# Wider filler matmuls, two feed-forward passes moved earlier in the second chunk, and three passes of a second product moved ahead of a between-product

## The chip, the cores and the metric

The kernel runs on one core of a Trainium2 chip. The metric is the device time of one execution in microseconds (us). The engines are PE (TensorE, with its weight loads shown apart as PEld), DVE (VectorE), ACT (ScalarE), POOL (GpSimd) and SP (SyncE, which here only issues DMAs).

## The reference, cut to what matters

There are 4 batches, 8 heads, 768 tokens and 48 dimensions a head. A delta-rule attention runs over the tokens; its outputs, 384 wide, go through a feed-forward layer with 2048 hidden columns, two slopes instead of a plain ReLU, and 384 output columns. Everything is float32.

```python
k_n = k / (norm(k) + 1e-06)
for t in range(S):
    kt, vt, bt = k_n[:, :, t], v[:, :, t], beta[:, :, t, None]
    y[:, :, t] = einsum('bhd,bhde->bhe', q[:, :, t], state)
    v_old = einsum('bhde,bhd->bhe', state, kt)
    state = state + bt[..., None] * einsum('bhd,bhe->bhde', kt, vt - v_old)
h = x @ w_in                                  # x: y as (3072, 384)
g = maximum(h, 0) + alpha * minimum(h, 0)
out = g @ w_out
```

## The kernel before, in words

**Tiling.** The tokens are cut into 12 chunks of 64. One *step* handles one chunk of one pair of batches, so there are N = 24 steps, numbered from 0: steps 0 and 1 are the first chunk, 2 and 3 the second, 4 and 5 the third. Inside a chunk the recurrence is solved as a triangular system. Its 64 x 64 inverse is built of 32 x 32 blocks: DVE inverts the diagonal blocks of four steps (NJ = 4) at once by elimination (`eliminate`, lines 516 and 522, with transposes by `turns`, line 489), ACT places them (`placing`, lines 642, 648 and 659) into the tiles `diag` and `inv`, and PE multiplies them together in two *between-products*: `between_1`, whose result ACT copies into `mid`, and `between_2`, which completes `inv` (lines 709 and 722 for the second chunk, where a DVE add, line 729, reads the second product out of PSUM; line 674 from step 4 on, where ACT copies, line 686).

**A step's other work.** `flips` transposes keys and queries on PE (line 377; ACT copies them out, line 398). `grams` multiplies keys with keys (line 424; DVE scales them, line 430). `through_state` (763), `query` (748), `solve` (788), `outputs` (801), `next_state` (817) and `to_ffn` (840) follow, with DVE reading most results. These products use a ring of three double PSUM banks, `p_pair`, in turn (`ps_big`): a product that comes to a bank waits until the last reader of what was there is done.

**Feed-forward.** Once a chunk's two steps are done, `ffn_in(c)` makes the hidden tiles (line 931): 48 matmuls a chunk, three to a hidden tile of 128 columns, two hidden tiles to one of two PSUM banks `p_ffn`. After every sixth matmul ACT (line 941) and DVE (two instructions, line 943) apply the slopes. `ffn_out(c)` is the second product for chunks 0 and 1 (line 973): two halves u of 128 tokens, each the sum of 16 matmuls f of 384 columns in one `p_ffn` bank, copied out by ACT (line 979) and stored. These are generators: each `next` issues one matmul, here called a *pass*. In the trace a float32 matmul leaves two records.

**Order.** All engines' order is the order in which the program writes the work (`manual_schedule`); `weave` interleaves generators by shares, and each engine takes its instructions in that order. Places that matter here:

- `busy` (line 1391) issues filler matmuls into an unused PSUM bank: the operands are the identity and a transposed-key tile `k_t[3]`, 112 rows of each. Their results are read by nothing. They stand where PE would wait: `busy(8)` ahead of the first chunk's elimination result, shorter ones within `first_chunk`.
- `second_pair` does steps 2 and 3, with `alongside(p, ...)` issuing p passes of `ffn_in(0)` and some weight conversions between its products. Weights come in by DMA as 32-bit words and are rebuilt by ACT (225, 226) and DVE (235, 240).
- After `second_pair`: `ffn_in(1)` beside `eliminate(1)`; then `ffn_out(0, True)`, whose two halves take turns; then a `weave` of `prelude(4)` (both between-products of step 4), `catch_up` (grams and flips of steps 10 and 11) and the first 8 passes of `ffn_out(1)`; then two rounds of `attention(n)`, n = 4 and 5, each with 12 more passes.
- From step 6 (`JOINED`) on, the rest of the feed-forward (`tail`) fills PE between the attention products up to the end.

Of the kernel before, what the change touches and what calls it, by code (L numbers as in the profile page):

```python
# [36 lines left out]
EARLY = 8  # L37
FIRST = 6
# [5 lines left out]
def kernel(  # L44
# [18 lines left out]
    FT = DFF // 128  # L63
# [17 lines left out]
    def ps_one():  # L81
        return ps_big()[:, 0]
# [17 lines left out]
    def ps_ffn():  # L100
        turn[0] ^= 1
        return ffn_banks[turn[0]]

    def half(i):
        return slice(64 * i, 64 * i + 64)
# [5 lines left out]
    ROWS = C + D  # L111
# [4 lines left out]
    def padded(name, n):  # L116

        ts = [const.tile([128, H, C], FP32, name=f"{name}{i}") for i in range(n)]
        for t in ts:
            nc.gpsimd.memset(t[:, :, D:C], 0.0)  # L120
        return ts

    NKE, NKL, NQ = 3, 2, 2
    ident = const.tile([128, 128], FP32, name="ident")
    make_identity(nc, ident)
    k_early, k_late, q_pad = padded("ke", NKE), padded("kl", NKL), padded("qp", NQ)
# [12 lines left out]
    def load_early(n, *queues):  # L139
        if n < N:  # L140
            fetch(k, n, early(n)[:, :, 0:D], *queues)
# [189 lines left out]
    stats, k_t, q_t, a_t = {}, {}, {}, {}  # L331
# [76 lines left out]
    def now(pieces):  # L408
        for x in pieces:
            x()  # L410
# [40 lines left out]
    NJ = 4  # L451
# [174 lines left out]
    def placing(n, parts, by_vector=False):  # L626


        if n >= N:
            return  # L630
        m, j = n // NJ, n % NJ
        first, second = slice(0, HB), slice(HB, C)
        own = slice(j * H, j * H + H)

        def put(dst, cols, src, i):
            out, x = dst[n % NE][:, :, cols], src[m][:, own]
            if by_vector:
                nc.vector.tensor_scalar(
                    out=out, in0=x, scalar1=which[:, i : i + 1], scalar2=None, op0=ALU.mult
                )  # L640
            else:
                nc.scalar.mul(out, x, which[:, i : i + 1])  # L642

        if 0 in parts:
            if n < NJ:
                put(diag, first, turned, 0)
            else:
                nc.scalar.copy(diag[n % NE][:, :, first], turned[m][:, own])
            yield
        if 1 in parts:  # L650
            put(inv if n >= NJ else diag, second, inverse, 1)
            yield
        if 2 in parts:
            put(inv, first, inverse, 0)
            yield
        if 3 in parts:
            w = stats[n][1]
            for t in range(2):
                nc.scalar.copy(w[half(1 - t), 2], w[half(t), 1])
            yield  # L660
# [300 lines left out]
    def ffn_out(c, together=False):  # L961

        gs = gss.pop(c)
        p_o = {}
        if together:
            order = [(u, f) for f in range(FT) for u in range(2)]
        else:
            order = [(u, f) for u in range(2) for f in range(FT)]
        for u, f in order:
            assert len(out_done) > f  # L970
            if f == 0:
                p_o[u] = ps_ffn()[:, 0:DM]
            nc.tensor.matmul(
                p_o[u], gs[f // 2][:, f % 2, u * 128 : (u + 1) * 128], w_out[:, f],
                start=(f == 0), stop=(f == FT - 1),
            )
            if f == FT - 1:
                o_sb = work.tile([128, DM], FP32, name="o_sb")
                nc.scalar.copy(o_sb, p_o[u])
                store(c, u, o_sb)  # L980
            yield
# [299 lines left out]
    IN_PARTS, OUT_PARTS, FAST_PARTS = FT * KT, NB * FT, 7 * FP // 2  # L1281


    def part(gen, n):
        for _ in range(n):
            next(gen, None)
            yield

    def weave(*gens):

        live = []
        for i, (g, n, *at) in enumerate(gens):
            at = at[0] if at else 0.0
            live.append([at, i, (1.0 - at) / n, g])
        while live:
            live.sort(key=lambda x: (x[0], x[1]))
            at = live[0]
            at[0] += at[2]
            try:
                next(at[3])  # L1300
            except StopIteration:
                live.pop(0)
# [83 lines left out]
    def busy(n, p=None):  # L1386

        p = ps_one() if p is None else p
        while n > 0:
            x = p[:, 0 : int(512 * min(n, 1))]  # L1390
            nc.tensor.matmul(  # L1391
                x, ident[0:ROWS],
                k_t[NJ - 1].rearrange("p g i -> p (g i)")[0:ROWS, 0 : x.shape[-1]],
            )
            n -= 1

# [103 lines left out]
    fetch_out, _, conv_out = weights(pieces, stages, ids, out_done)  # L1500
    PARTS_OUT = 2 * len(pieces)

    def chain(*gens):
        for g in gens:
            yield from g
# [46 lines left out]
    def alongside(products, pieces, *gens):  # L1552
        weave((part(first_in, products), products), (part(convert_on, pieces), pieces), *gens)

    def second_pair():

        n = 2
        both, x = (n, n + 1), NJ
        halves = [cross(0, slice(i * H, i * H + H), edge, half_way) for i in both]
        squares(x)  # L1560
        alongside(4, 2)
        for h in halves:
            next(h)
        flips(x, n)
        load_early(x + NKE)
        load_q(n + 2)
        squares(x + 1)
        alongside(5, 2)
        next(halves[0])
        flips(x + 1, n + 1)  # L1570
        load_early(x + 1 + NKE)
        load_q(n + 3)
        now(weigh(x))
        place(n, (0,))
        alongside(4, 2)
        next(halves[1])
        now(weigh(x + 1))
        place(n + 1, (0,))
        alongside(4, 2)
        for i in both:  # L1580
            now(between_1(i))
        now(grams(x))
        squares(x + 2)
        alongside(5, 3, (chain(*(placing(i, (1, 2, 3)) for i in both)), 6))
        for i in both:
            now(between_2(i))
        now(grams(x + 1))
        for i in both:
            scale_v(i)
        flips(x + 2, N)  # L1590
        load_early(x + 2 + NKE)
        now(weigh(x + 2))
        alongside(5, 3)
        y = ps_big()
        pieces = []
        for i in range(2):
            pieces += through_state(n + i, None, y[:, :, i * G * D : (i + 1) * G * D])
        now(pieces)
        squares(x + 3)
        alongside(5, 3)  # L1600
        y = ps_big()
        pieces = []
        for i in range(2):
            pieces += solve(n + i, y[:, :, i * G * D : (i + 1) * G * D])
        now(pieces)
        now(grams(x + 2))
        flips(x + 3, N)
        load_early(x + 3 + NKE)
        now(weigh(x + 3))
        alongside(5, 2)  # L1610
        pieces = []
        for i in both:
            y = ps_big()
            pieces += outputs(i, y[:, :, 0 : G * D]) + next_state(i, y[:, :, G * D : 2 * G * D])
        now(pieces)
        for i in both:
            load_late(i + 2)
            load_v(i + 3)
        alongside(5, 2)
        for i in both:  # L1620
            to_ffn(i)
        now(grams(x + 3))
        alongside(IN_PARTS - 42, 1)

    second_pair()
    fetch_out(len(stages))
# [15 lines left out]
    def prelude(n):  # L1642
        place(n, (0,))
        now(between_1(n))
        yield
        place(n, (1, 2))
        yield
        now(between_2(n))
        yield
        place(n, (3,))  # L1650
        scale_v(n)
        place(n + 1, (0,))
        yield

    def catch_up():
        for n in range(FIRST + NJ, EARLY + NJ):
            now(grams(n))
            flips(n + 1, N)
            squares(n + 1)
            yield  # L1660
            now(weigh(n + 1))
            load_early(n + 1 + NKE)
            yield

    late = ffn_out(1)
    few = OUT_PARTS // 4
    weave((prelude(NJ), 4), (catch_up(), 2 * (EARLY - FIRST), 0.1), (part(late, few), few))

    def feed_forward():
        for c in range(2, FAST_IN):  # L1670
# [26 lines left out]
    for n in range(NJ, JOINED):  # L1697
        extra = [] if n == NJ else [(weight_sums(0, 0, 3), 3)]
        weave(
            (attention(n), SHARES), (placing(n + 1, (1, 2, 3)), SHARES * PLACING),  # L1700
            (part(late, (OUT_PARTS - few) // 2), (OUT_PARTS - few) // 2),
            (part(blocks, share), share), *extra,
        )

    PIECES_OF = {JOINED: (2, 3, 2 * PIECES), JOINED + 1: (4, 4, 7)}
    TURNS = [(3, 3, 4), (3, 3, 4), (4, 4, 4), (0, 5, 6)]
    FILL = {JOINED: (8, 12, 12), JOINED + 1: (10, 12, 10), JOINED + 2: (8, 10, 12)}
# [2 lines left out]
    for n in range(JOINED, N):  # L1710
        if n == LATE:
            banks(2, 2)
        fill, share = FILL.get(n, FILLS[n % 2]), PIECES_OF.get(n, TURNS[n % NJ])
        extra = [[], [], []]
# [72 lines left out]
```

## Time and profile before

| what | us |
|---|---|
| runs | 666.2, 670.96, 676.8; median 670.96 |
| profiled execution, whole | 664.06 |
| profiled execution, span | 662.3 |
| PE busy in the span | 641.2 |
| mean granted TensorE clock over the span | 0.994 |
| DVE busy / ACT busy | 492.2 / 264.8 |

Times within the trace count from the start of the span. A profile line of the timeline has start, length, engine, source line, operation, output and inputs, and how many instructions were merged; in square brackets is the idle time of the engine before it and what ended that. The windows view gives for each stretch the busy time of each engine, the granted clock and the DMA share.

### The profile page before, as it was taken

What the parts mean: (1) busy time and instruction counts of PE and PEld (TensorE: products, weight loads), DVE (VectorE), ACT (ScalarE), POOL (GpSimd) and SP (SyncE); (2) the same over time, 40 slices, a digit from 0 to 9 for tenths busy, and PEclk for the clock granted to TensorE, in tenths of its full rate; (3) what the DMA queues carried; (4) which work ended last, traced back from release to release, by engine and by line L of the source; (5) the groups of instructions that cost most, each with busy time, mean ns of one, the idle gap of its engine ahead of it and who ended that gap; (6) DMA issues with size and microseconds to landing.
All of it is one profiled execution on the core that took longest, in us unless ns stands there. A gap on an engine that the chain in (4) does not pass through costs nothing.

```text
span 662.3 us, 22128 instructions
## 1 busy us (share of the span) xinstructions
PE 641.2 (97%) x9551; PEld 567.0 (86%) x9551; DVE 492.2 (74%) x1180; ACT 264.8 (40%) x621; POOL 93.7 (14%) x201
## 2 busy tenths in 40 slices
PE   4999999989999999999999999999999999999997
PEld 3578888557688998998998998988999999999997
DVE  5955889868999859748859758858968658567383
ACT  5937765245454343243343233232245245042140
POOL 6000122001000000001000000000035044062260
PEclk9799999999999999999999999999999999999999
DMA  8848845211422122122111111112111210100000
GB/s 121 245 126 218 199 87 144 49 37 38 78 58 50 21 55 50 26 50 51 26 38 37 27 38 37 26 38 38 26 42 34 44 32 2 31 9 2 24 1 25
DMA packets 110962, 37.72 MB, mean 57 GB/s; under 512 B 104160, under 2 KB 107248, under 8 KB 110864
## 3 DMA queue, kind: packets, MB, share of 16 engines
q1 hardware_dynamic: 109088, 35.81, 24.8%
q8 instruction: 75, 1.23, 0.8%
q10 hardware_dynamic: 1776, 0.49, 0.4%
q14 instruction: 23, 0.19, 0.1%
HBM read 31.56 MB, written 4.72 MB: 55 GB/s over the span
## 4 chain that ended last, share of the span: by engine, by line
PE 83%; DVE 10%; ACT 3%; SPq 2%; issue 1%; DMA 0%; DVEq 0%; ACTq 0%
PE p_ffn L931 22%; PE p_ffn L995 17%; PE p_more L1247 8%; PE p_more L1163 4%; PE p_ffn L1153 3%; PE p_ffn L1247 3%; PE p_pair L377 2%; PE p_ffn L1158 2%; PE p_pair L763 2%; PE p_pair L788 2%; PE p_pair L674 2%; PE p_pair L801 2%; DVE prod L516 2%; DVE block L522 2%; PE p_pair L1391 2%; PE p_pair L424 1%
## 5 line engine op out<-in xcount | busy, mean ns | idle before, releaser
L931 PE MATMUL p_ffn<-xt,w_in 128*128 128x256 f32 x768 | 175.1, 382 | 2.3 <-DVE act L943 1.2
L931 PEld LDWEIGHTS p_ffn<-xt,w_in 128*128 128x128 f32 x768 | 142.7, 190 | 22.7 <-issue 1.9
L943 DVE SCALAR_TENSOR_TENSOR act<-act,al_t,p_ffn 128x256 f32<-128x256 f32 x112 | 48.6, 476 | 29.3 <-ACT act L941 29.2
L941 ACT ACTIVATE act<-p_ffn 128x512 f32<-128x512 f32 x56 | 33.3, 594 | 81.3 <-PE p_ffn L931 81.2
L522 DVE TENSOR_TENSOR block<-block,prod 128x30 f32<-128x30 f32 (+9 forms) x150 | 49.9, 333 | 5.2
L1187 POOL TENSOR_TENSOR k_t<-k_t 128x128 f32<-128x128 f32 (+1 forms) x48 | 29.5, 615 | 166.6 <-ACT k_t L1182 164.1
L516 DVE TENSOR_TENSOR prod<-block 128x30 f32<-128x30 f32 (+9 forms) x150 | 49.0, 326 | 1.8
L995 PE MATMUL p_ffn<-w_out,act 128*128 128x192 f32 x288 | 49.6, 328 | 0.1
L995 PEld LDWEIGHTS p_ffn<-w_out,act 128*128 128x128 f32 x288 | 46.5, 190 | 0.8 <-issue 0.5
L842 ACT COPY xt<-p_pair 128x384 f32<-128x384 f32 x22 | 10.4, 478 | 91.2 <-PE p_pair L840 77.5
L366 POOL TENSOR_TENSOR beta_t<-beta_t,rec 128x8 f32<-128x8 f32 x24 | 6.3, 261 | 284.6 <-DVE rec L364 264.7
L1187 POOL TENSOR_TENSOR block<-block 128x128 f32<-128x128 f32 (+1 forms) x48 | 27.9, 582 | 16.7 <-ACT block L1182 14.2
L1153 PE MATMUL p_ffn<-xt,w_in 128*128 128x256 f32 x96 | 28.7, 380 | 0.0
L773 DVE TENSOR_TENSOR r<-v_raw,p_pair 64x192 f32<-64x192 f32 (+1 forms) x66 | 23.2, 352 | 1.1
L686 ACT COPY inv<-p_pair 32x256 f32<-32x256 f32 x40 | 14.5, 362 | 23.9 <-DVE u L792 23.6
L792 DVE TENSOR_TENSOR u<-p_pair,wgt 128x384 f32<-128x384 f32 x24 | 13.3, 557 | 14.3 <-PE p_pair L674 14.0
L1201 DVE SCALAR_TENSOR_TENSOR act<-block,al_t,act 128x256 f32<-128x256 f32 x32 | 19.1, 637 | 5.2 <-ACT block L1197 5.1
L1015 DVE TENSOR_TENSOR o_sb<-u,p_ffn 128x192 f32<-128x192 f32 x24 | 7.9, 351 | 20.2 <-PE p_ffn L995 19.7
L1247 PE MATMUL p_more<-w_out,act 128*128 128x192 f32 x128 | 21.9, 329 | 0.0
L642 ACT ACTIVATE inv<-inverse,which 128x256 f32<-128x256 f32 x44 | 21.6, 503 | 0.3
L1182 ACT COPY k_t<-p_more 128x512 f32<-128x512 f32 x16 | 9.4, 586 | 30.6 <-PE p_more L1163 25.9
L752 ACT COPY y<-p_pair 128x384 f32<-128x384 f32 x22 | 10.4, 478 | 27.5 <-PE p_pair L748 25.5
(224 smaller groups left out, 1415.5 us busy)
## 6 DMA issues: line engine op xcount, KB each, us to landing
w_out<-in_moe_w_in_dram SPq DMA_DIRECT2D x12, 512.0 KB, 5.2
qp<-in_q_dram SPq DMA_DIRECT2D x48, 96.0 KB, 3.0
v_raw<-in_v_dram SPq DMA_DIRECT2D x48, 96.0 KB, 2.9
kl<-in_k_dram SPq DMA_DIRECT2D x96, 48.0 KB, 2.8
out_dram<-o_sb SPq DMA_DIRECT2D x92, 48.0 KB, 1.6
space_out<-in_moe_w_out_dram SPq DMA_DIRECT2D x11, 384.0 KB, 5.2
ke<-in_k_dram SPq DMA_DIRECT2D x43, 96.0 KB, 3.3
w_out<-in_moe_w_out_dram SPq DMA_DIRECT2D x5, 384.0 KB, 4.0
```

The lines of the kernel that those rows point to most:

```text
L516: nc.vector.tensor_tensor(out=prod, in0=r[:, 0:j, j : j + 1].to_broadcast([128, j, n]), in1=r[:, j : j + 1, j + 1 : HB].to_broadcast([128, ...
L522: nc.vector.tensor_tensor(out=r[:, 0:j, j + 1 : HB], in0=r[:, 0:j, j + 1 : HB], in1=prod, op=ALU.add)
L642: nc.scalar.mul(out, x, which[:, i : i + 1])
L773: nc.vector.tensor_tensor(out=r[to, a], in0=v_in[to, a], in1=p[own, a, :, 0:D], op=ALU.subtract)
L931: nc.tensor.matmul(p_h[:, i], w_in[:, t, (f + i) * 128 : (f + i + 1) * 128], xt[:, t], start=(t == 0), stop=(t == KT - 1),)
L941: nc.scalar.activation(g, p_h, ACT.Relu, scale=-1.0)
L943: nc.vector.scalar_tensor_tensor(out=g[:, i], in0=g[:, i], scalar=al_t[:, f + i : f + i + 1], in1=p_h[:, i], op0=ALU.mult, op1=ALU.add,)
L995: nc.tensor.matmul(p, x(i), w(i), start=(i == 0), stop=(i == FP - 1))
L1153: nc.tensor.matmul(p[:, f * 256 : f * 256 + 256], w(2, f), xt[:, 2], start=True, stop=False)
L1163: nc.tensor.matmul(q[:, j], a, b, start=True, stop=True)
L1187: nc.gpsimd.tensor_tensor(out=dst, in0=a, in1=b, op=ALU.add)
L1247: nc.tensor.matmul(p, x(i), w(i), start=(i == 0), stop=(i == FP - 1))
```

## The change

Four edits. The fillers read all 128 rows of the identity and of `k_late[0]`, the tile that holds the keys of step 0 (and later of the even steps) for `next_state`. In `second_pair` seven passes instead of five stand between `between_1` and `between_2` of steps 2 and 3, and two fewer at its end. `ffn_out(0, True)` takes its last four matmuls in the order (half 0, f 14), (half 0, f 15), (half 1, f 14), (half 1, f 15). Three passes of `ffn_out(1)` are issued ahead of `prelude`, `prelude` gives way one time fewer (the placing of `inv` now follows `between_1` at once), and the two rounds of attention get 11 passes each instead of 12; the last of all 33 calls only ends the generator.

```diff
@@ ffn_out
         if together:
-            order = [(u, f) for f in range(FT) for u in range(2)]
+            order = [(u, f) for f in range(FT - 2) for u in range(2)]
+            order += [(u, f) for u in range(2) for f in range(FT - 2, FT)]
@@ busy
             nc.tensor.matmul(
-                x, ident[0:ROWS],
-                k_t[NJ - 1].rearrange("p g i -> p (g i)")[0:ROWS, 0 : x.shape[-1]],
+                x, ident, k_late[0].rearrange("p h d -> p (h d)")[:, 0 : x.shape[-1]]
             )
@@ second_pair
-        alongside(5, 3, (chain(*(placing(i, (1, 2, 3)) for i in both)), 6))
+        alongside(7, 3, (chain(*(placing(i, (1, 2, 3)) for i in both)), 6))
...
-        alongside(IN_PARTS - 42, 1)
+        alongside(IN_PARTS - 44, 1)
@@ prelude
         now(between_1(n))
-        yield
         place(n, (1, 2))
@@
-    few = OUT_PARTS // 4
-    weave((prelude(NJ), 4), (catch_up(), 2 * (EARLY - FIRST), 0.1), (part(late, few), few))
+    few, rest = OUT_PARTS // 4, 11
+    for _ in part(late, OUT_PARTS - few - 2 * rest + 1):
+        pass
+    weave((prelude(NJ), 3), (catch_up(), 2 * (EARLY - FIRST), 0.1), (part(late, few), few))
@@ attention rounds
-            (part(late, (OUT_PARTS - few) // 2), (OUT_PARTS - few) // 2),
+            (part(late, rest), rest),
...
+    assert next(late, None) is None
```

## The prediction

> **What bounds the kernel now.** I read the page's busy times first, then PE's waits, then the windows, then the timeline around the edited places.
>
> ```profile
> PE 641.2 (97%) x9551; PEld 567.0 (86%) x9551; DVE 492.2 (74%) x1180; ACT 264.8 (40%) x621; POOL 93.7 (14%) x201
> ```
>
> PE has 21.1 us of idle time in 662.3, of which 8.8 lie in the first 16 us (the windows view: 7.19 busy). The waits from there on that matter are in PE's list (total us, times, longest):
>
> ```profile
> PE p_pair L674 <- ACT diag L648: 1.4, 1, 1.4
> PE p_ffn L931 <- DVE act L943: 1.2, 1, 1.2
> PE p_pair L840 <- DVE y L807: 1.1, 1, 1.1
> PE p_pair L674 <- ACT inv L642: 0.9, 1, 0.9
> PE p_pair L722 <- ACT diag L642: 0.9, 2, 0.7
> ```
>
> The change aims at the first (step 4's first between-product), the fourth (its second) and the fifth (steps 2 and 3): 1.36, 0.89 and 0.65 + 0.22 us. That is 3.1 us, the most that the moved passes can fill. The windows (length, busy us of PE, PEld, DVE, ACT, POOL, clock, DMA) say who sets the pace behind them:
>
> ```profile
> 20.00:22.00 2.00, 2.00 (x3) 0.90 (x4) 1.74 (x7) 2.00 (x5) 0.00 (x0) 0.50 1.03 420
> 24.00:26.00 2.00, 2.00 (x6) 0.81 (x6) 1.72 (x8) 1.93 (x5) 0.00 (x0) 1.00 1.27 234
> ...
> 75.00:97.00 22.00, 22.00 (x413) 18.99 (x404) 18.67 (x46) 14.10 (x32) 3.29 (x8) 1.00 0.64 174
> ...
> 165.00:190.00 25.00, 23.45 (x392) 17.42 (x391) 23.12 (x58) 12.48 (x33) 0.56 (x2) 1.00 0.44 84
> 190.00:215.00 25.00, 23.65 (x350) 20.55 (x350) 24.62 (x56) 11.29 (x29) 2.55 (x4) 1.00 0.24 43
> 215.00:240.00 25.00, 25.00 (x435) 23.77 (x436) 18.86 (x55) 7.65 (x20) 1.41 (x4) 1.00 0.21 41
> ```
>
> PE alone sets 75 to 97. From 165 to 215 it is **DVE**, busy 47.7 of 50 us, and PE's two waits there (1.1 and 1.2) are for DVE. From 215 on it is PE. The timeline of steps 2 and 3:
>
> ```profile
> 65.04 2.42 PE L931 MATMUL p_ffn<-xt,w_in 128*128 128x256 f32 x10
> ...
> 68.11 1.12 PE L722 MATMUL p_pair<-diag,mid 64*64 64x32 f32 x32 [0.65 <-ACT diag L642]
> ...
> 69.35 0.42 DVE L729 TENSOR_TENSOR inv<-diag,p_pair 128x256 f32<-128x256 f32 x1 [0.67 <-PE p_pair L722]
> ...
> 69.81 0.40 ACT L659 COPY wgt<-wgt 64x4 f32<-64x4 f32 x2
> ...
> 71.00 0.65 PE L377 MATMUL p_pair<-ident,ke 128*112 128x128 f32 x4
> ...
> 72.65 0.58 ACT L941 ACTIVATE act<-p_ffn 128x512 f32<-128x512 f32 x1
> ...
> 73.83 0.86 DVE L943 SCALAR_TENSOR_TENSOR act<-act,al_t,p_ffn 128x256 f32<-128x256 f32 x2
> ```
>
> To be seen: L377 follows L729 in the PSUM bank, and L941 with its two L943 now comes after both.
>
> [...] with 256 columns the fillers of 112 rows have a median of 431 ns, the hidden matmuls of 128 rows a mean of 382. [...] PE idles 3.43 us up to 16.06 (for `al_sb`), the clock is 0.50 from 17.5 to 22, then 1.00 from 24 on. [...]
>
> **Part A, fillers of 128 rows: 0.** Same number, same columns. The first filler now waits for the four loads of `k_late[0]`: issued from 10.69 to 14.15, landing at most 4.0 us after issue, so by 18.2; it starts at 19.73. The last filler (to 46.8) now holds back the reload of that tile, where L817 (to 44.4) did; but SP is issuing weights until 49.43 and comes to that load at 49.52. Both covers hold. Unknown is the clock in executions that were not profiled; see the rivals.
>
> **Part B, seven passes: +0.3.** A pass of L931 takes 0.43 us (14 records in 3.29 against 10 in 2.42). Two fill the idle 0.65 before L722 and push it to about 68.3. The second L722 is released by ACT at 69.4 as before, so its 0.22 goes too. At the end of the following grams, 71.0, PE has done two passes more: −0.87. But 4 + 5 + 4 + 4 + 7 = 24 passes end the fourth bank, so L941 and two L943 are now issued here, ahead of both L729. ACT reaches L941 when the last L659 ends, 69.81 + 0.40 = 70.21, to 70.8; L943 takes 0.87, to 71.7; the first L729 ends at 72.1 instead of 69.77. L377 waits for it: 72.15 instead of 71.00, +1.15. Sum +0.28. Who is behind the waiting L729: the grams' L430, L737 and `through_state`'s L773, about 0.8 late; `solve` (L788, 78.70) moves to 79.9 and finds them done near 79.2. PE is full up to 97, so +0.3 is carried; `flips` at 115.05, and through ACT and DVE the elimination from 119.55, move with it. Bounds: −0.87 (no new wait) to +1.2 (nothing filled).
>
> **Part C, three passes ahead of step 4: −0.3.** A pass of L973 takes 0.65 (64 records, 32 passes, in 20.93). Three take 1.95 where 1.36 is idle, so the first L674 starts 0.6 late. They need the bank of half 0: with the new order its last matmul ends two passes (1.3) before the end, and the 0.48 copy is done in time; by the old order the copy ended at 137.16, about when PE came free, so the reordering is worth 0 to 0.1. The removed yield puts the placing of `inv` (2 x 0.45) right behind the `mid` copies (0.74) on ACT instead of behind L477, L398 and L347: done at about 141.6, while PE comes near 143.3, so the 0.89 goes. Net −0.3 at the second grams (145.68). From there L430, ACT L477 and the L489 transposes of the next elimination move by −0.3, and DVE's dense queue carries just that to 209. Whatever PE gains beyond it in 150 to 209, it waits out: three passes fewer in the two rounds leave up to 1.95 of holes at L788, L801 and the step-6 products. On SP the four stores of half 0 go ahead of the `kl` load for step 6 (158.96): some 1.5 us late, needed at 200.10. Bounds: −2.25 (both waits gained, nothing given back) to +0.6.
>
> **Sum.** 0 + 0.3 − 0.3 = 0 against the profiled execution: span 662.3, whole 664.1. That execution lies 6.9 below the median of 670.96 and below all three runs; the mean of the four is 669.5. No view shows what the others lose. I predict **670 us**, between mean and median.
>
> **Rivals.**
> - *A warmer clock.* The cold stretch costs: L593 starts at 28.62, behind slow fillers, though its transposes ended at 26.48, so 2.1 us. If the other executions have more such stretches and 128 rows prevent them, up to the 6.9 go: 664 to 668. For: the spread of 10.6 us. Against: from 24 on the clock was 1.00 with 112 rows[...]. 0.12.
> - *All idle gained.* B gives −0.87, C −2.25: 670 − 3.1 = 667. For: the waits are real. Against: DVE at 95% behind them. 0.13.
> - *Slower: the slopes jam DVE.* L943 ahead of L729 is one mechanism: every 0.1 that ACT is later at L941 than 70.2 is 0.1 on L377. It decides from 69.9 on, where B turns from gain to loss. If ACT's weight rebuilding pushes L941 to 71.5, B is +1.6, and the late L773 takes L788 with it, another 1: 670 + 2.6 = 672.6, and with C's holes not absorbed (+0.6) 673. 0.17.
> - *Cold fillers.* [...] the 20.4 us of PE work between 28 and 50 run at half clock, +13 or more: 683. 0.03.
>
> **Numbers.** Forecast 0.55, the rivals as given. The forecast's own range is the spread of the runs, about 666 to 676, with ±1 for the bounds: 665 to 677. To hold eight in ten over all cases I take 663 to 678. A measurement of this kernel tells about 2%, 13.4 us, from no change; only the cold rival reaches that: faster 0.03, same 0.92, slower 0.05.
>
> **What would show it.** B: L943 before L729, L377 idle about 1.2 for L729, no wait at the first L722. C: no wait at either L674 near 139 to 143, a longer wait at L788 or L801 between 163 and 180, the wait at 208 still there. A: clock 1.00 from 24 on. The prediction is wrong if PE's idle sum falls by over 2 us, or if the clock row differs.

## The result and the profile after

| | before | after |
|---|---|---|
| median of 20 runs each, us | 670.22 (664.22 to 676.89) | 666.76 (663.75 to 670.88) |
| ratio, 95% interval | | 0.9977 [0.9958, 0.9996] |
| profiled execution, whole / span | 664.06 / 662.3 | 665.83 / 664.1 |
| from the start to the first L931 | 48.09 | 49.67 |
| from the L931 ahead of L722 (steps 2 and 3) to the L377 of the third chunk near 92 | 26.73 | 26.87 |
| from the first L973 to the first L995 (974 and 996 after) | 96.13 | 95.64 |
| from there to the end | 449.81 | 449.86 |

No difference of 2%; the forecast of 670 (663 to 678) holds. The interval of the ratio, 0.04 to 0.42%, is 0.3 to 2.8 us. Ratios leave out runs over 1.5% longer than the fastest of their kernel (4 of E8's 22, 2 of E3's 14), while medians hold all runs.

The last four rows are read from the timeline as differences between the first instructions of a line. The edits of parts B and C show in the rows of 26.73 and of 96.13 us. The stretch from the L377 near 92 us to the first L973 and the one from the first L995 to the end repeat to 0.1 us in all the traces taken here. The row of 26.73 is less steady, since stretches at half the clock (in E3 the clock is 0.82 from 64 to 68 us and 0.75 from 68 to 72) and stalls (idle time of PE for which the profile names no cause, 1.15 us in E3) can fall into it; its pieces, in the section on E6, are steady. The span of the changed kernel is longer only because it was 2.1 us late at 67 us, ahead of parts B and C (1.6 of it at the first L931).

PE's list of waits, after (total us, times, longest):

```profile
PE p_ffn L931 <- ACT beside L400: 1.5, 1, 1.5
...
PE p_ffn L931 <- DVE act L943: 1.2, 1, 1.2
PE p_pair L788 <- DVE a_t L444: 1.1, 2, 0.8
PE p_pair L377 <- DVE inv L729: 0.9, 1, 0.9
...
PE p_pair L801 <- DVE u L792: 0.7, 1, 0.7
...
PE p_pair L840 <- DVE y L807: 0.5, 1, 0.5
```

The two waits of L674 and that of L722 are gone. In their place stand L377 for L729, L788 and L801 for DVE, and the first line, L931 for the copy L400 of ACT, at 190.65 us: it was 0.25 before and is 1.54 now. L931 for L943 and L840 for L807 are old ones. The timeline of steps 2 and 3, after (L722 has no bracket left):

```profile
67.16 3.29 PE L931 MATMUL p_ffn<-xt,w_in 128*128 128x256 f32 x14
...
70.38 2.26 PE L722 MATMUL p_pair<-diag,mid 64*64 64x32 f32 x61
...
72.24 0.59 ACT L941 ACTIVATE act<-p_ffn 128x512 f32<-128x512 f32 x1
...
72.86 0.87 DVE L943 SCALAR_TENSOR_TENSOR act<-act,al_t,p_ffn 128x256 f32<-128x256 f32 x2 [2.06 <-ACT act L941]
73.64 0.75 DVE L729 TENSOR_TENSOR inv<-diag,p_pair 128x256 f32<-128x256 f32 x2
74.12 0.65 PE L377 MATMUL p_pair<-ident,ke 128*112 128x128 f32 x4 [0.92 <-DVE inv L729]
```

DVE sat idle for 2.06 us. The first L722 had ended at about 71.5, but L729, which reads its result, stood in DVE's queue behind L943, and L943 waited for L941. Both L729 come after it, and L377 after them. Step 4, after:

```profile
139.24 2.10 PE L974 MATMUL p_ffn<-w_out,sums 128*128 128x384 f32 x6
...
141.27 0.69 PE L674 MATMUL p_pair<-diag,right 32*32 32x32 f32 x32
...
142.78 0.91 ACT L642 ACTIVATE inv<-inverse,which 128x256 f32<-128x256 f32 x2
...
145.24 0.69 PE L674 MATMUL p_pair<-inv,mid 32*32 32x32 f32 x32
```

Three passes stand ahead of the first L674, and ACT has placed `inv` 1.5 us before the second one comes. What follows, in windows with the columns as before:

```profile
165.00:190.00 25.00, 22.17 (x443) 16.69 (x435) 22.80 (x58) 10.85 (x29) 1.12 (x4) 1.00 0.40 75
190.00:215.00 25.00, 23.02 (x344) 19.84 (x345) 24.62 (x55) 13.02 (x34) 2.55 (x4) 1.00 0.26 49
```

From 165 to 215 DVE is as busy as it was (47.42 of 50 us). PE's idle time there is 2.83 + 1.98 = 4.81 us, and was 1.55 + 1.35 = 2.90: 1.91 more, nearly the 1.95 of the three passes that were taken from there. The largest piece of it is the wait of L931 for ACT. ACT stands behind DVE there: its copy L477 waits for DVE's L430, and L400 follows in ACT's order.

```profile
187.61 0.82 ACT L477 COPY same<-right 32x256 f32<-32x256 f32 x2 [3.45 <-DVE right L430]
...
189.96 0.60 ACT L400 COPY beside<-p_pair 112x512 f32<-112x512 f32 x1
...
190.65 3.69 PE L931 MATMUL p_ffn<-xt,w_in 128*128 128x256 f32 x16 [1.54 <-ACT beside L400]
```

L430 comes 1.77 us later than before (186.83 against 185.06), and L931 1.77 later (190.65 against 188.88): PE has less to do ahead of it, but comes no sooner than DVE lets it.

### The profile page after: what moved, and what is told of

Read it like the earlier page. It is cut to its first block, busy times and chain, and to the rows that moved or that the text cites. A ratio compares the mean times of both kernels' runs of the same rounds, so it can differ in the third digit from the quotient of the medians.

```text
span 664.1 us, 22126 instructions
## 1 busy us (share of the span) xinstructions
PE 643.9 (97%) x9551; PEld 568.9 (86%) x9551; DVE 493.3 (74%) x1180; ACT 264.0 (40%) x621; POOL 93.2 (14%) x201
## 4 chain that ended last, share of the span: by engine, by line
PE 86%; DVE 7%; ACT 4%; issue 1%; DMA 1%; ACTq 0%; SPq 0%; DVEq 0%
PE p_ffn L931 22%; PE p_ffn L996 17%; PE p_more L1248 8%; PE p_more L1164 4%; PE p_ffn L974 4%; PE p_ffn L1154 3%; PE p_ffn L1248 3%; PE p_pair L377 3%; PE p_ffn L1159 2%; PE p_pair L763 2%; PE p_pair L788 2%; PE p_pair L801 2%; PE p_pair L424 2%; PE p_pair L674 2%; PE p_pair L1392 2%; PE p_pair L748 1%
## 5 line engine op out<-in xcount | busy, mean ns | idle before, releaser
L931 PE MATMUL p_ffn<-xt,w_in 128*128 128x256 f32 x768 | 175.1, 382 | 3.6 <-ACT beside L400 1.5
L931 PEld LDWEIGHTS p_ffn<-xt,w_in 128*128 128x128 f32 x768 | 142.7, 190 | 24.0 <-ACT beside L400 1.9
L943 DVE SCALAR_TENSOR_TENSOR act<-act,al_t,p_ffn 128x256 f32<-128x256 f32 x112 | 48.6, 476 | 30.4 <-ACT act L941 30.3
L941 ACT ACTIVATE act<-p_ffn 128x512 f32<-128x512 f32 x56 | 33.3, 595 | 81.0 <-PE p_ffn L931 80.8
L1016 DVE TENSOR_TENSOR o_sb<-u,p_ffn 128x192 f32<-128x192 f32 x24 | 7.9, 352 | 20.2 <-PE p_ffn L996 19.8
L349 DVE TENSOR_REDUCE norm<-ksq 128x8 f32<-128x384 f32 x24 | 13.0, 547 | 12.5 <-ACT ksq L347 12.4
L1202 DVE SCALAR_TENSOR_TENSOR act<-k_t,al_t,act 128x256 f32<-128x256 f32 x32 | 21.7, 718 | 0.1
```

What stands on the lines that cost most here:

```text
L931: nc.tensor.matmul(p_h[:, i], w_in[:, t, (f + i) * 128 : (f + i + 1) * 128], xt[:, t], start=(t == 0), stop=(t == KT - 1),)
L941: nc.scalar.activation(g, p_h, ACT.Relu, scale=-1.0)
L943: nc.vector.scalar_tensor_tensor(out=g[:, i], in0=g[:, i], scalar=al_t[:, f + i : f + i + 1], in1=p_h[:, i], op0=ALU.mult, op1=ALU.add,)
L1202: nc.vector.scalar_tensor_tensor(out=g[:, f], in0=r[:, f], scalar=al_t[:, 2 * i + f : 2 * i + f + 1], in1=g[:, f], op0=ALU.mult, op1=ALU.add,)
```

## The experiments

Twelve kernels. E1 to E4 take the parts one by one, E6, E7, E8, E11 and E12 alter the changed kernel, E5, E9 and E10 turn to what the fillers' rows do. The kernel before was run beside them in three sets: medians 667.77 (59 runs), 667.17 (43) and 667.23 (57). None of them shows the 670.22 of the first set again, and the 666.76 of the changed kernel lies 0.4 to 1.0 us below them where the first set had 3.5; but it was not run again beside them.

### E1 to E4: the parts alone

**E1**, part A: only the operands of `busy` changed.

> The kernel before with the 128-row fillers alone. Theory of the record [...]: ratio to before 1.000, within 0.002, and the same spread of times and granted clocks as before. Rival (wider fillers wake the clock sooner, which is where the 0.23% of the whole change came from): ratio near 0.998, the mean granted clock of the runs higher than that of before, no run above 672 us.

**E2**, parts B and C: everything but the operands of `busy`.

> The whole change but the fillers, which keep 112 rows. Theory of the record, with the sizes of the two traces: seven passes +0.1 to +0.3 us, passes ahead of step 4 -0.3 to -0.5 us, together -0.4 to 0: ratio 0.9994 to 1.000. Rival (all of the gain is in the moves): ratio near 0.9977, -1.5 us.

**E3**, part B: only the two counts of `alongside`.

```diff
-        alongside(5, 3, (chain(*(placing(i, (1, 2, 3)) for i in both)), 6))
+        alongside(7, 3, (chain(*(placing(i, (1, 2, 3)) for i in both)), 6))
...
-        alongside(IN_PARTS - 42, 1)
+        alongside(IN_PARTS - 44, 1)
```

> Only the seven passes between the between-products of steps 2 and 3. Theory: the new wait of L377 for L729 (about 0.9 to 1.2 us) takes back the filled idle time (0.87): +0.1 to +0.3 us, ratio 1.000 to 1.0005. Rival (the fill pays and the wait is hidden): -0.9 us, ratio 0.9987, and no wait of L377 for L729 in the profile.

**E4**, part C: `ffn_out`'s order, `prelude` without its first yield, three passes ahead, 11 in each round.

> Only the passes ahead of step 4, with the reordered end of the product before and the shorter prelude; fillers of 112 rows, five passes in step 2 and 3. Theory: both waits of L674 (1.4 and 0.9 us) are gone from the profile, new waits of L788 and L801 for DVE of 1 to 2 us stand between 163 and 180, net -0.3 to -0.5 us, ratio 0.9993 to 0.9996. Rival (both waits are gained and nothing is given back): -2.25 us, ratio 0.9966.

| | ratio, 95% interval | median | L931 to L377 | L973 to L995 |
|---|---|---|---|---|
| E1: A | 0.9995 [0.9965, 1.0024] | 668.29 | 27.30* | 96.73* |
| E2: B and C | 0.9985 [0.9961, 1.0009] | 667.08 | 27.54* | 95.71 |
| E3: B | 0.9963 [0.9931, 0.9995] | 666.93 | 27.36* | 96.10 |
| E4: C | 0.9988 [0.9961, 1.0016] | 666.87 | 26.74 | 95.65 |

\* a stretch at half the clock lies in this segment.

The ratios can't tell the parts apart. E3's lies further below 1 than that of the whole change, and its interval leaves 1 out, though none of its segments holds a gain. So one interval without 1 among twelve is no proof of a gain here. The segments can: C alone is worth 95.65 − 96.13 = −0.48, and in E2 it is −0.42. B can't be read from this segment in E2 or E3, where half-clock stretches fall into it. For A the profile of E1 says more than its ratio:

```profile
19.64 7.13 PE L1391 MATMUL p_pair<-kl,ident 128*128 128x512 f32 x16
27.93 1.57 PE L593 MATMUL p_pair<-turned,sums 32*32 32x16 f32 x128 [1.15 <-DVE turned L489]
29.42 1.97 PE L1391 MATMUL p_pair<-kl,ident 128*128 128x512 f32 x2
```

Sixteen records took 7.13 us, 0.45 each, at the full clock; the next two took 1.97. The window of 28 to 32 us has a clock of 0.70, that of 32 to 36 one of 0.50: it fell at about 29.6, when PE had waited 1.15 us for L489 and run the 128 small products of L593 (1.57 us). Fillers of 128 rows did not prevent that.

### E6: six passes instead of seven

```diff
-        alongside(7, 3, (chain(*(placing(i, (1, 2, 3)) for i in both)), 6))
+        alongside(6, 3, (chain(*(placing(i, (1, 2, 3)) for i in both)), 6))
...
-        alongside(IN_PARTS - 44, 1)
+        alongside(IN_PARTS - 43, 1)
```

> The whole change with six passes between the second chunk's between-products instead of seven, the seventh given back to the stretch after the grams. 4 + 5 + 4 + 4 + 6 = 23 passes do not end the fourth bank, so L941 and L943 stay behind the L729. Theory (the two ends of step B cancel: 0.87 idle filled, about the same lost to the wait of L377 for L729): no wait of L377 for L729, 0.2 to 0.3 us left at the L722, and the stretch from the L931 ahead of that L722 to the second chunk's L377 near 92 us takes 26.2 to 26.4 us, against 26.73 before and 26.87 with seven. Rival (PE loses the 0.4 elsewhere, by ACT or DVE): 26.7 or more. The ratio of the whole changes by less than 0.1%.

Ratio 0.9987 [0.9960, 1.0014], median 667.37. Its timeline:

```profile
65.96 2.86 PE L931 MATMUL p_ffn<-xt,w_in 128*128 128x256 f32 x12
...
69.04 1.12 PE L722 MATMUL p_pair<-diag,mid 64*64 64x32 f32 x32 [0.22 <-ACT diag L642]
...
71.93 0.65 PE L377 MATMUL p_pair<-ident,ke 128*112 128x128 f32 x4
```

L377 has no wait left, and each of the two groups of L722 waits 0.22. From the L931 to L377 it takes 5.97 us, as before, with one pass more in it. The segment took 26.62, above the expected 26.2 to 26.4. The ten records of L931 ahead of L840 put 0.3 into it (2.73 us, 2.43 before), with such a stall of 0.43 in their weight loads; E8 and E12 with the same six passes took 26.31 and 26.29.

Stalls and half-clock stretches come and go in this segment (seven passes took 26.87 in the change, but 27.30 in E7 and 29.07 in E11). Two pieces of it hold what the passes change, and they repeat wherever no half-clock stretch falls into them:

| passes | traces | L931 to L377 | L840 to the next L377 |
|---|---|---|---|
| 5 | before, E4, E5, E9, E10 | 5.93 to 5.97 | 4.50 |
| 6 | E6, E8, E12 | 5.94 to 5.97 | 4.07 |
| 7 | change, E7, E11 | 6.94 to 6.96 | 3.63 to 3.64 |

So six passes gain 0.4 where seven lose 0.1: the seventh, which closes the bank and calls L941 and L943, costs 0.55 net.

### E7 and E11: what carries part C

**E7** is the changed kernel with the yield of `prelude` put back:

```diff
         now(between_1(n))
+        yield
         place(n, (1, 2))
...
-    weave((prelude(NJ), 3), (catch_up(), 2 * (EARLY - FIRST), 0.1), (part(late, few), few))
+    weave((prelude(NJ), 4), (catch_up(), 2 * (EARLY - FIRST), 0.1), (part(late, few), few))
```

> The whole change with the yield of the prelude put back (and its weight of 4), so that ACT places the inverse behind the others' work again. Theory (of step C's 0.48 us the second L674's wait is the larger part): the second L674 waits 0.3 to 0.9 us for ACT's L642, and the stretch from the first L973 to the first L995 takes 95.9 to 96.1 us, against 95.64 with the change and 96.13 before. Rival (the passes ahead of step 4 alone bring it, or DVE's dense queue behind takes back whatever is gained here): 95.6 to 95.7.

Ratio 1.0011 [0.9985, 1.0038], median 667.65. The timeline of ACT and of the second L674 in E7:

```profile
147.93 0.82 ACT L477 COPY same<-right 32x256 f32<-32x256 f32 x2 [1.66 <-DVE right L430]
148.77 0.58 ACT L398 COPY k_t<-p_pair 112x512 f32<-112x512 f32 x1
149.38 0.52 ACT L347 ACTIVATE ksq<-ke 128x384 f32<-128x384 f32 x1
149.81 0.89 ACT L642 ACTIVATE inv<-inverse,which 128x256 f32<-128x256 f32 x2
150.35 0.69 PE L674 MATMUL p_pair<-inv,mid 32*32 32x32 f32 x32 [0.89 <-ACT inv L642]
```

The wait is back at 0.89, and the segment takes 96.52: 0.88 more than with the change, and 0.39 more than before. That is beyond both expectations. The moved passes without the yield's removal lose, and removing the yield gains 0.88 on top of them, as the pieces show:

| from, to | before | E7 | change |
|---|---|---|---|
| L973, first L674 | 22.29 | 22.68 | 22.67 |
| first L674, L763 of step 4 | 10.17 | 10.17 | 9.22 |
| L763, L377 near 160 | 11.45 | 11.46 | 11.55 |
| L377, first L995 | 52.22 | 52.21 | 52.20 |

The removal without the moved passes was not run; by these pieces it would be worth about 0.9, an estimate.

**E11** is the changed kernel with `ffn_out`'s old order.

```diff
-            order = [(u, f) for f in range(FT - 2) for u in range(2)]
-            order += [(u, f) for u in range(2) for f in range(FT - 2, FT)]
+            order = [(u, f) for f in range(FT) for u in range(2)]
```

> The whole change with the old order of the second product's matmuls, halves in turn to the end, the three passes still ahead of step 4. Theory (the copy of half 0 must end before the next bank is free; with the old order it ends about when PE comes free): the stretch from the first L973 to the first L995 is 95.64 as with the change or up to 0.1 longer. Rival (the reordering carries part of step C): 95.9 or more, with a wait of the first L974 of step 4's three passes for the copy.

Ratio 0.9992 [0.9965, 1.0018], median 667.33; the segment took 95.82, 0.18 more than with the change, all of it ahead of the first L674 (22.86 against 22.67). The weight load of step 4's first pass waits 0.54 us for L979, the copy of half 0, as the rival had it. The size lies between the two expectations: the reordering is worth somewhat more than the 0 to 0.1 that was forecast for it, and does not carry the step.

### E5, E9 and E10: do the rows of a filler count?

The kernel before with 32, 64 and 96 rows in place of 112; columns and counts stay.

```diff
-                x, ident[0:ROWS],
-                k_t[NJ - 1].rearrange("p g i -> p (g i)")[0:ROWS, 0 : x.shape[-1]],
+                x, ident[0:32],
+                k_t[NJ - 1].rearrange("p g i -> p (g i)")[0:32, 0 : x.shape[-1]],
```

> The kernel before with fillers of 32 rows instead of 112, columns and number as they were. Theory [...]: a filler's record is about 0.43 us at the full clock and 0.85 at half, the mean granted clock of the timed runs stays at the 0.991 of the kernel before and the median within 1.5 us of it. Rival [...]: with 32 rows the fillers run cold throughout, the mean granted clock falls to 0.985 or less and the median rises by 3 us or more.

> The kernel before with fillers of 64 rows. With 32 rows sixteen fillers took 14.02 us, half the clock throughout, and PE was slow up to about 57 us; with 112 they took 9.0 with a change to the full clock near 24 us. Theory (the clock opens from some share of rows on, and 112 lies well above it): with 64 rows the fillers change to the full clock as with 112, the sixteen take 8.5 to 10 us, the median is within 2 us of the kernel before. Rival (the share counts by degrees, so that each row brings the opening nearer): 11 to 14 us for the sixteen and a median of 672 or more; then 128 rows in place of 112 could be worth something too.

> The kernel before with fillers of 96 rows. Theory (112 is well above the point from which rows count): as before, sixteen fillers in 8.5 to 10 us, median within 2 us. Rival (112 is just at that point, and 16 rows more or less decide): over 11 us, half-clock stretches up to 50 us in the profile, median 672 or more.

| rows | kernel | median | ratio, 95% interval |
|---|---|---|---|
| 32 | E5 (6 runs) | 682.40 | 1.0220 [1.0171, 1.0268] |
| 64 | E9 (4 runs) | 682.85 | 1.0207 [1.0156, 1.0257] |
| 96 | E10 (20 runs) | 672.96 | 1.0065 [1.0042, 1.0087] |
| 112 | before | 667.2 to 667.8 | |
| 128 | E1 | 668.29 | 0.9995 [0.9965, 1.0024] |

The theory behind E5, the author's assumption that rows count for nothing, fell. So did that of E9, that 64 rows do as well as 112, and that of E10, that 96 do as well too. In E5 the timeline of PE has

```profile
20.00 14.02 PE L1391 MATMUL p_pair<-k_t,ident 32*128 32x512 f32 x16
...
59.99 1.07 PE L817 MATMUL p_pair<-u,kl 64*64 64x48 f32 x32
60.99 0.76 PE L1391 MATMUL p_ffn<-k_t,ident 32*128 32x256 f32 x2
```

The sixteen records take 0.88 us each, twice the 0.45 of E1. L817 still takes 1.07 for its 32, where the kernel before needs 0.65 to 0.68; the last line, two records of 256 columns in 0.76, is the first that comes near the time of the kernel before (0.70), and the pair at 56.25 still took 1.22 (the expectation of E9 puts the change at 57). PE was busy for all of 20 to 60 us. The clock column does not tell of it:

```profile
24.00:28.00 4.00, 4.00 (x6) 1.49 (x5) 3.55 (x14) 3.87 (x8) 0.00 (x0) 1.00 1.02 167
```

It shows 1.00, and so does the mean clock of that execution (1.000): only the durations tell. With 64 rows the sixteen fillers take 14.02 us as well, and PE is slow for longer: the eight L931 records at 64.16 take 3.78 us, where the eight of E5 at 63.18 take 1.99. With 96 they take 9.95 and the clock is 1.00 from 28 to 36 us, but it is lost again from about 37.2 to 54.3 (windows of E10; the clock is the third number from the end):

```profile
32.00:36.00 4.00, 4.00 (x130) 2.65 (x126) 0.70 (x2) 2.81 (x5) 0.00 (x0) 1.00 0.59 108
36.00:40.00 4.00, 4.00 (x136) 2.46 (x134) 2.04 (x6) 0.51 (x1) 0.00 (x0) 0.65 0.78 188
```

PE is busy for 4.00 of every 4 us there, and the clock goes from 1.00 to 0.50. It is no single case: the mean clock of E10's runs is 0.981, that of the kernel before beside them 0.993. So PE was busy throughout in E5 and E9 (20 to 60 us) and in E10 (20 to 52) and was slow all the same, and all that their edits change is the rows of the fillers. Whether they count by degrees, as E9's rival had it, stays open: sixteen fillers of 32 and of 64 rows took 14.02 us, of 96 rows 9.95, and 96 still cost 0.65%. From 112 (8.96 us) to 128 nothing more is to be measured (0.9995).

### E8 and E12: fewer fillers

Six passes as in E6, and in E8 also

```diff
-BUSY = 8
+BUSY = 6
```

which shortens the one block ahead of L593 from 16 records to 12; E12 has `BUSY = 7`, 14 records.

> The whole change with six passes as above and the constant BUSY at 6 instead of 8, so that a quarter of the fillers ahead of and among the first steps goes. Theory (fillers at half the clock hold back the first L593 by 1 to 2 us[...]): the first L593 starts 1 to 2 us earlier, and the median lies 0.5 to 2 us below the change's. Rival (the fillers keep the clock up): more half-clock records in the first 50 us, a mean granted clock below 0.993 and a median above the change's.

> The whole change with six passes between the between-products and the constant BUSY at 7, so that 14 fillers stand ahead of the first L593 instead of 16 (12 with 6). With 12 PE idled 1.82 us for L489 ahead of L593 and ran at half the clock from 28 to 50 us; with 16 it had no idle there. Theory (14 end about when the last transpose does, so that no idle is left and the clock stays): first L593 at 27 to 28.5 us, mean granted clock as with the change (0.994 or more), median 0.5 to 1 us below the change's. Rival (each filler taken away costs clock): mean granted clock between 0.985 and 0.992, median at 668 or more.

E8: ratio 1.0008 [0.9976, 1.0040], median 671.00, mean clock over its runs 0.985. Its rival held:

```profile
18.86 6.52 PE L1392 MATMUL p_pair<-kl,ident 128*128 128x512 f32 x12
27.20 1.56 PE L593 MATMUL p_pair<-turned,sums 32*32 32x16 f32 x128 [1.82 <-DVE turned L489]
```

L593 starts 2.4 us earlier than after the change, PE idles 1.82 us for it, and the clock is half from 28 to about 52 us. E12: ratio **0.9956 [0.9931, 0.9981]**, median 665.73, mean clock 0.996:

```profile
20.28 8.05 PE L1392 MATMUL p_pair<-kl,ident 128*128 128x512 f32 x14
28.38 1.42 PE L593 MATMUL p_pair<-turned,sums 32*32 32x16 f32 x128
```

L593 comes 1.2 us earlier and without idle time, as the theory had it; the median is 1.0 below the change's. E12 has the lowest median of the study. Its ratio is 0.44% below 1 and its interval leaves 1 out, but E3 shows how little one such interval proves. By the segments, six passes and part C make 0.9 us of it (0.13%). The rest would have to lie ahead of the first L931, which comes at 48.59 in this trace; with sixteen fillers it comes at 48.09 before, 47.80 in E3, 48.67 in E6 and 49.67 after the change. So that 14 fillers are better than 16 is not shown, nor that E12 is faster than the change, whose interval overlaps its own.

## Why the prediction was right, and where it was not

**The bound.** That PE sets the pace except from 165 to 215, where DVE does, held: what the moved passes left there came back as 1.91 us of idle PE. The prediction looked for it at L788, L801 and the step-6 products; the largest piece is the L931 behind ACT at 190.65.

**Part A, forecast 0; E1 ratio 0.9995.** The first filler did not wait for its load, as forecast. The number was right and its ground was not. The prediction set the warmer-clock rival aside since the clock was 1.00 from 24 us on with 112 rows, and it took for granted that the number of rows does not count; that was the author's assumption, which no trace had shown. The runs speak against it: with PE busy for all of 20 to 52 us, 32 and 64 rows cost 2% (E5, E9), 96 rows 0.65% (E10). Part A is worth nothing because 112 and 128 both come out the same, not because rows don't count. That 112 was already enough was luck. The prediction also read the half clock before as 17.5 to 22 us, where the trace has it from 16.6 to 23.4 (the windows read 0.81 for 16 to 17 us, 0.50 up to 23, 0.78 for 23 to 24). And its last sign of being wrong, a clock row that differs, did appear: the row reads 0.50 at 20 us before and 1.00 after. It was a poor sign, since the sixteen fillers under the 1.00 took 9.48 us, longer than the 8.96 before. Its other sign did not come: PE's idle sum fell by 0.9, from 21.1 to 20.2, and the first 16 us, ahead of every edit, hold more than that (8.8 to 6.8).

**Part B, forecast +0.3; measured 26.87 − 26.73 = +0.14.** The same +0.1 stands in the pieces of three traces with seven passes. The mechanism is the one forecast: the idle before L722 filled, a new wait of L377 for L729 behind L943 and L941. Its term was mis-sized: 1.15 forecast, 0.92 measured. Counted from the L931, L377 started 0.15 earlier than forecast (74.12 − 67.16 against 72.15 − 65.04), because L941, L943 and L729 each came 0.1 to 0.15 earlier, and PE was free for it 0.08 later. That L729 would be held back behind L943 was the author's estimate; the trace shows it: DVE is idle for 2.06 us ahead of L943, with L729 behind it. The second half of the slopes rival did not come: from L377 to the L788 of step 2 it takes 7.70 us in both kernels.

**Part C, forecast −0.3; measured −0.49, and −0.48 alone.** Its terms were +0.6 for the first L674 and −0.9 for the second. Measured: +0.38 (22.67 − 22.29), −0.95 (9.22 − 10.17) and +0.1 on the stretch behind. The first was priced too high, by 0.2, for the new order that it assumed. In E11, with the old order, it is 0.57 (22.86 − 22.29), but that holds a wait for the copy that the forecast did not have, so that the two agree is chance; the reordering, priced at 0 to 0.1, is worth that 0.19. That the later rounds give nothing back held. What the prediction did not draw from its own two terms is that the passes only cost: E7 shows that they lose 0.39 on their own, since they put off the first L674, and what they save later lies in DVE's stretch. The gain is that of the yield's removal.

**The sum and the median.** The edits sum to +0.14 − 0.49 = −0.35 us, forecast 0. The ratio says −1.5 [−2.8, −0.3], which just holds −0.35; the rest belongs to no edit that the experiments found. The range of 663 to 678 was as wide as the spread of the runs, so that the median lies in it says little for the parts; the segments do.

Lines fitted through the runs' times and their mean clocks give the same time where the clock reads 1.00, 665.5 ± 0.4 for the change and 665.5 ± 0.4 for the kernel before (59 runs), with 3.7 us for each 0.01 of clock. So the larger difference of the first set probably lies in the clock; it is not shown, as the clocks of that set's runs of the kernel before are not on record, and the reading does not show slow records that stand under a clock of 1.00. Whether parts B or C make high clocks likelier stays open: the runs of E1 have a mean of 0.993, E3 0.995, E4 0.994, those of the kernel before 0.991, 0.992 and 0.993 in the three sets. The last section has two traces in which a wait that these parts take away or bring stands ahead of a half-clock stretch.

**The rivals.** All idle gained fell with C's holes and B's wait; cold fillers did not come, since the first filler has no idle time ahead of it in any trace and so did not wait for `k_late[0]`; the warmer clock fell as a gain (0.9995 with 128 rows), but fewer rows than 112 cost 0.65 to 2.2%.

## What to carry to other kernels

Before idle time of PE is filled with moved work, see which engine sets the pace where that work came from: here it was DVE, and 1.91 us of idle time came back for the 1.95 that were taken away. Moving what that idle time waits for, here one placing earlier in ACT's queue, gained 0.88 and was the better edit. Count the passes up to the end of a bank: the one pass that closes it brings the slopes of two other engines with it, and here six passes gained 0.4 us where seven lost 0.1. Try fillers of many rows: here sixteen of 32 or 64 rows took 14.02 us and the kernel over 2% longer, sixteen of 112 rows 8.96. Of the three lengths tried, the short one that left PE idle for 1.82 us had the highest median; between the other two nothing is shown.

## What the runs showed of the hardware that was not expected

In E10 a half-clock stretch began at about 37 us with PE busy for 4.00 of every 4 us from 20 to 52, there with matmuls of 32 rows (L610) and fillers of 96. With fillers of 112 or 128 rows there are nine half-clock stretches after the first 25 us (E1 three, E2 two, E3, E7, E8 and E11 one each), and each has an idle time of PE of 0.62 to 1.82 us at its start or up to 2.7 us ahead of it. Five of these are a stall of L424 (1.45 in E1, 1.27 in E2, 1.15 in E3) or L709 (1.18 in E2, 0.62 in E7) for which the profile names no cause, two are L593's wait for L489 (1.15 in E1, 1.82 in E8), and two are waits that this change is about:

```profile
144.40 0.69 PE L674 MATMUL p_pair<-diag,right 32*32 32x32 f32 x32 [1.47 <-ACT diag L648]
145.02 1.09 PE L973 MATMUL p_ffn<-w_out,sums 128*128 128x384 f32 x2
```

```profile
72.56 1.10 PE L377 MATMUL p_pair<-ident,ke 128*112 128x128 f32 x4 [0.92 <-DVE inv L729]
```

The first is E1, the wait that part C removes: the L424, L377 and L973 behind it take 1.13, 1.10 and 2.61 us, the next ones, from 152.05 on, 0.69, 0.65 and 2.10, the page's row of the clock shows 8 tenths for 134 to 150 us and 9 on both sides, and the segment takes 0.6 us more. The second is E11, the wait that part B brings: the clock is 0.57 in the window of 72 to 76 us, and from L377 to L788 it takes 9.19 us instead of 7.71. So in these two traces 0.6 and 1.48 us came on top of the wait itself. The same waits left the clock at 1.00 in the trace of the kernel before (1.36) and in that of the change (0.92), so idle time alone does not decide either; what does is not shown.

The clock column reads 1.00 over fillers of very different length: the sixteen took 7.13 us in E1, 9.48 in the trace of the change and 14.02 in E5, the last two at mean clocks of 0.999 and 1.000. So in these traces a mean clock near 1 does not rule out a slow first 30 to 60 us.

In the traces, nearly all of what two executions differ by beyond the edits has its place ahead of the third chunk's L377 (at 92 us in the trace before): from there to the first L973 they differ by 0.05, from there to the first L995 by no half-clock stretch but that of E1 (0.6), and from L995 to the end by 0.1.
